# Fused dilated sliding-window attention and GEGLU block: loads, output copies, masks and the first gate stage put in another order

## The chip, the core and the metric

The kernel runs on one core of a Trainium2 chip. The core has five engines with an instruction stream each: TensorE (PE in the profile, its weight loads PEld), VectorE (DVE), ScalarE (ACT), GpSimd (POOL) and SyncE (SP), which here only issues transfers. Each works through its stream in order and waits on semaphores for the others. The metric is the device time of one execution in microseconds (us).

## What is computed

For 8 batches and 8 heads of 576 positions with head size 64, a softmax attention is taken in which a query sees only a few keys: heads 0 to 3 ("plain") the last 32 positions, heads 4 to 7 ("dilated") every fourth of the last 128. The result, 4608 tokens by 512, goes through a gated feed-forward block.

```python
rel = pos[:, None] - pos[None, :]
mask_plain = (rel >= 0) & (rel < 32)
mask_dil = (rel >= 0) & (rel < 128) & (rel % 4 == 0)
scores = np.where(mask, q @ k.T / 8, -1e9)
attn = softmax(scores);  x = attn @ v            # x: 4608 x 512
out = (gelu(x @ w_gate) * (x @ w_val)) @ w_out   # 512 -> 1536 -> 512
```

## The kernel before, in words

The whole order is written by hand (`manual_schedule`): each engine runs its instructions in the order in which the code names them, and the frame only adds the semaphore waits.

**Attention units.** A unit `n` is a pair of heads of one batch, four units to a batch: `n // 4` is the batch, units 0 and 1 of a batch are plain, 2 and 3 dilated. A unit has three steps. `emit_s` computes the scores on PE into four PSUM banks starting at `b0`, then ACT takes the exponential into a tile `P` (L329 and L330 for a plain unit, L345 for a dilated one). The mask is applied in one of two ways: with `pe_mask=True`, PE first adds a bias of 0 or -60000 by four matmuls with the identity (L315, L335); otherwise `emit_s` hands back a function that multiplies `P` by a 0/1 mask on DVE (L353). `emit_pv` computes, on PE, the numerators and the denominators (L435; `den` and `num` do the two apart). `norm_r` (transpose L440, reciprocal L442, transpose L444) makes the reciprocals on DVE, and `norm_x` (L455 plain, L458 dilated) writes the unit's 128 rows of x, transposed, into `xT[n % 4]`.

**Feed-forward chunks.** The 4608 tokens are nine chunks of 512. Chunk `c` first runs twelve column blocks `nb` of `ffn1`: four matmuls for the gate, four for the value (L470), one for each of the four `xT` tiles; `geglu` then takes the gelu on ACT (L495) and the product on DVE (L496). The first two blocks of chunks 0 to 2 go through `ffn1_two`, which in the kernel before runs `xT[0..2]` for both blocks (gate and value) and then `xT[3]` for all four sums (L483). Then come four token blocks of `ffn2`, twelve matmuls each (L502), whose sums `store` copies to SBUF (`osb`, L513 on ACT) and sends out (L517 on SP). `osb` has four buffers. `hooks` put attention steps between the matmuls of an `ffn2`.

**PSUM.** Eight banks. `mm0` (0, later 4) is the first of the four banks of the feed-forward, `SB = 4 - mm0` the first of the four in which scores are made, `V = mm0 + 1` the first bank of a unit's numerators and denominators in chunks 0 to 2. All scores of a chunk use the same four banks, so a unit's scores wait until the exponential of the unit before them has read its own.

**Which unit where.** `in_a` gives the units whose `emit_pv` lies among the `ffn1` blocks of a chunk, `in_b` those whose scores lie from the last `ffn1` block on. The scores of batch 2 lie in chunk 1, those of batches 3 and 4 in chunks 1 and 2, and of batch `c + 2` at the end of chunk `c` from chunk 3 on. Units 20 and 24, the first of batches 5 and 6, thus open the `ffn2` part of chunks 3 and 4.

**Loads.** `load_batch` of a batch issues, on SP, 15 loads of q, k (L183) and v (L171), then seven DMA transposes ("the crossbar": L212, L213, L217) into `qTd` and `qTp`; and on POOL, loads of the dilated part (L196 to L206) and the casts to 16 bits (L188, L189, L175, L176) that the transposes wait for. SP works in order, so transposes that wait for a cast hold up all that stands behind them, outputs too. The tile `st`, and the 16-bit copies `qp`, `qd` and `rd`, have one buffer each. Batches 0 and 1 come another way: their q and k are transposed on PE (`t_plain` L258, `t_dil` L279 and L289) and copied out of PSUM (L243 ACT, L247 DVE).

Of the kernel before, what the change touches and what calls it, by code (L numbers as in the profile page):

```python
# [37 lines left out]
def kernel(  # L38
# [436 lines left out]
    def ffn1_two(c, pairs):  # L475

        tok = slice(c * CH, (c + 1) * CH)
        for kcs in (range(NKC - 1), (NKC - 1,)):
            for nb in range(2):
                ns = slice(nb * P, (nb + 1) * P)  # L480
                for gi, w in ((0, wg_t[0]), (1, wv_t[0])):
                    for kc in kcs:
                        nc.tensor.matmul(  # L483
                            ps[:, pairs[nb] + gi, :],
                            w[:, kc, ns],
                            xT[kc][:, tok],
                            start=(kc == 0),
                            stop=(kc == NKC - 1),
                        )
# [63 lines left out]
    for hp in range(2):  # L553
        t_plain(0, q6, hp, 2 * hp, ("act", "dve"))
    copy("pool", qd0[:, 0], r4(first_d[0]))
    copy("dve", qd0[:, 1], r4(first_d[1]))
    nc.vector.tensor_scalar(bias_d, mask_d, 1.0, 60000.0, ALU.subtract, ALU.mult)
# [15 lines left out]
    emit_s(0, 4, pe_mask=True)  # L573
    emit_s(1, 0, pe_mask=True)
    warm(2, 7)
    t_dil(0, 0, qd0, first_r, 4, 0, ("dve", "dve", "dve"))
    t_dil(0, 1, qd0, first_r, 4, 1, ("act", "dve", "dve"))
    den(0, 5)
    emit_s(2, 0, pe_mask=True)
    den(1, 5)  # L580
# [32 lines left out]
    in_a = {2: ((3, 12), (7, 13)), **{c: tuple(zip((1, 3, 5, 7), range(NHP * (c + 1), NHP * (c + 2)))) for c in range(3, B - 1)}}  # L613
    in_b = {1: range(8, 14), 2: range(14, 20), **{c: range(NHP * (c + 2), NHP * (c + 3)) for c in range(3, B - 2)}}
    for c in range(NCH):
        if c == 1:
            load_batch_rest(2, *half2)
        if c >= 2 and c + 2 < B:
            load_batch(c + 2)
        pv_at = dict(in_a.get(c, ()))  # L620
# [6 lines left out]
        for nb in range(NNB):  # L627
# [4 lines left out]
            elif nb > 1 or c > 2:  # L632
                ffn1(c, nb, pairs[(nb + (c < 2)) % 2])
# [7 lines left out]
            if c == 0 and nb in (6, 7):  # L641
                t_plain(1, q61, nb - 6, 4 + 2 * (nb - 6), ("act", "dve"))
            if c == 0 and nb == 8:
                rr = rd1.rearrange("p t h r d -> p t (h r d)")
                for hp in range(2):
                    t_dil(1, hp, qd1, (rr[:, 0], rr[:, 1]), 4, hp, ("dve", "dve", "dve"))
# [124 lines left out]
```

## Time and profile before

| | us |
|---|---|
| three runs, lowest / median / highest | 378.22 / 379.12 / 382.39 |
| the profiled execution, device time | 378.81 |
| its span, first to last instruction | 377.0 |
| PE busy in it | 350.3 |
| DVE / ACT / POOL busy | 196.4 / 148.5 / 68.1 |

In PE's timeline the chunks' first matmuls stand at 26.1 us (chunk 0), 75.7 (1), 116.9 (2), 158.8 (3), 197.9 (4) and 238.9 (5). A row of the timeline has the start, the duration, the engine, the line, the operation, what it writes and reads, how many were merged, and in brackets how long the engine stood idle just before and which instruction or transfer ended that. Since matmuls overlap, the step of a stream of them is read from their starts: eight of an `ffn1` block take 1.73 us, twelve of an `ffn2` block 2.59.

### The profile page before, as it was taken

How to read it: one execution, taken by the hardware profiler on the slowest of the kernel's cores; microseconds unless marked ns; L12 is line 12 of the kernel's file. 1: busy time of each engine (PE TensorE's matmuls, PEld its weight loads, DVE VectorE, ACT ScalarE, POOL GpSimd, SP SyncE). 2: the span in 40 equal slices, each digit the busy share in tenths (PEclk: the TensorE clock that was granted, in tenths of full speed). 3: DMA queues.
4: the chain of work that ended last, by engine and by line, in shares of the span. 5: the costliest groups of instructions: out<-in, count | busy, mean ns of one | idle time of the engine just before them, and what ended most of it. 6: DMA issues, size and time to landing. Idle time of an engine off the chain costs nothing.

```text
span 377.0 us, 6546 instructions
## 1 busy us (share of the span) xinstructions
PE 350.3 (93%) x2644; PEld 168.0 (45%) x2644; DVE 196.4 (52%) x293; ACT 148.5 (39%) x209; POOL 68.1 (18%) x94
## 2 busy tenths in 40 slices
PE   5969898999979999799799979999999999999995
PEld 2544444444434444354344434444444444444442
DVE  3593434644487665579427942497359704312420
ACT  2532356143636245622463244523653213313321
POOL 2380504520620520025000520040000000000000
PEclk9898999999999999999999998999999999999999
DMA  8999999969994991189618981488110020011002
GB/s 208 221 172 230 159 201 188 183 126 189 192 182 127 179 150 60 54 191 140 81 57 198 157 112 56 125 176 103 57 57 0 2 83 30 0 57 57 0 28 83
DMA packets 101565, 44.04 MB, mean 117 GB/s; under 512 B 76768, under 2 KB 96752, under 8 KB 101536
## 3 DMA queue, kind: packets, MB, share of 16 engines
q1 hardware_dynamic: 82224, 30.69, 37.9%
q0 software_dynamic: 17776, 11.25, 23.2%
q10 hardware_dynamic: 1536, 1.70, 2.0%
q8 instruction: 20, 0.33, 0.4%
q14 instruction: 9, 0.07, 0.1%
HBM read 38.05 MB, written 9.44 MB: 126 GB/s over the span
## 4 chain that ended last, share of the span: by engine, by line
PE 58%; DMA 17%; SPq 12%; DVE 4%; issue 3%; POOL 3%; ACT 2%; ACTq 0%; POOLq 0%; DVEq 0%
PE ps L470 27%; PE ps L502 23%; SPq L217 6%; DMA qTp<-qp 5%; SPq L183 4%; DMA st<-in_k_dram 4%; PE ps L435 4%; DMA xT<-in_k_dram 3%; DMA sv<-in_v_dram 3%; DMA wv<-in_moe_w_val_dram 2%; PE ps L343 1%; PE ps L326 1%; SPq L171 1%; POOL vp L175 1%; DVE xT L458 1%
## 5 line engine op out<-in xcount | busy, mean ns | idle before, releaser
L495 ACT ACTIVATE g<-ps 128x512 f16<-128x512 f32 x108 | 64.0, 597 | 141.3 <-PE ps L470 129.9
L496 DVE SCALAR_TENSOR_TENSOR u_all<-g,ps 128x512 f16<-128x512 f16 x108 | 73.9, 687 | 81.9 <-PE ps L470 69.2
L470 PE MATMUL ps<-xT,wg 128*128 128x512 f16 x408 | 104.9, 379 | 1.5 <-ACT osb L513 1.3
L502 PE MATMUL ps<-wo,u_all 128*128 128x512 f16 x432 | 101.4, 384 | 4.1 <-ACT osb L513 2.1
L470 PE MATMUL ps<-xT,wv 128*128 128x512 f16 x408 | 104.7, 379 | 0.1
L502 PEld LDWEIGHTS <-u_all 128*128 128x128 f16 x432 | 40.2, 99 | 52.5 <-issue 7.4
L470 PEld LDWEIGHTS <-wv 128*128 128x128 f16 x408 | 39.9, 98 | 48.5 <-issue 0.4
L470 PEld LDWEIGHTS <-wg 128*128 128x128 f16 x408 | 38.1, 98 | 46.9 <-issue 2.3
L188 POOL CAST qp<-st 128x2048 f16<-128x2048 f32 x6 | 11.3, 1890 | 122.3 <-DMA st<-in_k_dram 92.1
L513 ACT ACTIVATE osb<-ps 128x512 f32<-128x512 f32 x30 | 17.9, 597 | 36.0 <-PE ps L502 36.0
L440 DVE STREAM_TRANSPOSE dt<-ps 128x576 f32<-128x576 f32 x32 | 25.0, 780 | 10.1 <-PE ps L435 9.9
L345 ACT ACTIVATE P<-ps 128x1280 f16<-128x1280 f32 x16 | 19.8, 1236 | 17.1 <-PE ps L343 17.1
L444 DVE STREAM_TRANSPOSE rb<-rc 128x576 f32<-128x576 f32 x32 | 24.9, 778 | 1.1
L353 DVE TENSOR_TENSOR P<-P,mask_p 128x1440 f16<-128x1440 f16 x12 | 11.4, 956 | 22.4 <-ACT P L330 22.4
L515 DVE TENSOR_SCALAR osb<-ps 128x512 f32<-128x512 f32 x6 | 4.1, 691 | 30.6 <-PE ps L502 30.6
L329 ACT ACTIVATE P<-ps 128x800 f16<-128x800 f32 x16 | 13.4, 837 | 16.3 <-PE ps L326 16.2
L458 DVE TENSOR_TENSOR xT<-ps,rb 128x576 f16<-128x576 f32 x16 | 17.9, 1124 | 1.4 <-PE ps L435 1.1
L353 DVE TENSOR_TENSOR P<-P,mask_d 128x1280 f16<-128x1280 f16 x12 | 9.9, 823 | 15.6 <-ACT P L345 15.6
L435 PE MATMUL ps<-P,ones 128*64 128x64 f16 (+4 forms) x320 | 15.2, 224 | 0.6 <-DVE qTd L247 0.4
L326 PE MATMUL ps<-qTp 64*128 64x160 f16 (+1 forms) x160 | 9.0, 237 | 5.1 <-DMA qTp<-qp 5.1
L455 DVE TENSOR_TENSOR xT<-ps,rb 128x576 f16<-128x576 f32 x16 | 12.0, 751 | 2.7 <-PE ps L435 2.5
L175 POOL CAST vp<-sv 128x1024 f16<-128x1024 f32 x8 | 9.0, 1125 | 14.4 <-DMA sv<-in_v_dram 14.4
(71 smaller groups left out, 233.0 us busy)
## 6 DMA issues: line engine op xcount, KB each, us to landing
out_dram<-osb SPq DMA_DIRECT2D x36, 256.0 KB, 2.0
sv<-in_v_dram SPq DMA_DIRECT2D x32, 128.0 KB, 3.6
st<-in_q_dram SPq DMA_DIRECT2D x24, 128.0 KB, 3.1
st<-in_k_dram SPq DMA_DIRECT2D x24, 128.0 KB, 3.5
qd<-in_q_dram POOLq DMA_DIRECT2D x7, 256.0 KB, 5.1
qd<-in_k_dram POOLq DMA_DIRECT2D x7, 256.0 KB, 6.6
vd<-in_v_dram POOLq DMA_DIRECT2D x7, 256.0 KB, 6.3
wg<-in_moe_w_gate_dram POOLq DMA_DIRECT2D x3, 512.0 KB, 6.4
```

What stands on the lines that cost most here:

```text
L217: nc.sync.dma_start_transpose(out=dst[:, :, kb * P : kb * P + n], in_=qp[0:n, kb].rearrange("p t h d -> p (t h d)"))
L345: nc.scalar.activation(pt, ps[:, b0 : b0 + 4, 0:DW], AF.Exp, bias=0.0, scale=scale)
L353: nc.vector.tensor_tensor(pt, pt, mb, ALU.mult)
L435: nc.tensor.matmul(o, lhs, rhs, start=st, stop=True, skip_group_check=True)
L440: nc.vector.transpose(dt.rearrange("p b c -> p (b c)"), den)
L444: nc.vector.transpose(rb.rearrange("p (b c) -> p b c", c=32), bass.AP(tensor=rc.tensor, offset=rc.offset, ap=[rc.ap[0], [1, 18], [0, 32]]),)
L458: nc.vector.tensor_tensor(dst.rearrange("p (i m s) -> p i m s", m=2, s=2), num, rb.rearrange("p (s m i) -> p i m s", s=2, m=2), ALU.mult,)
L470: nc.tensor.matmul(ps[:, b0 + gi, :], w[:, kc, ns], xT[kc][:, tok], start=(kc == 0), stop=(kc == NKC - 1))
L495: nc.scalar.activation(g, ps[:, b0, :], AF.Gelu)
L496: nc.vector.scalar_tensor_tensor(u_all[:, nb, :], g, USCALE, ps[:, b0 + 1, :], ALU.mult, ALU.mult)
L502: nc.tensor.matmul(ps[:, bank, :], u_all[:, fc, tb * P : (tb + 1) * P], wo_t[fc // 4][:, fc % 4, :], start=(fc == 0), stop=(fc == NNB - 1),)
L513: nc.scalar.activation(osb, ps[:, bank, :], AF.Copy, bias=0.0, scale=1.0 / USCALE)
```

## The change

- The start. `bias_d` is computed on POOL instead of DVE, ahead of POOL's cast of `qd0`; in the built program a row named ISA stands directly ahead of it. The cast of the dilated k of batch 0 moves from DVE to ACT, between the exponentials of units 0 and 1, and four of the copies of `t_dil` go to ACT where three were on DVE. `den(0, 5)` moves ahead of the `t_dil` calls, `den(1, 5)` behind them and ahead of the scores of unit 2; two warming matmuls go.
- `ffn1_two` runs each `xT[kc]` for all four sums before the next `kc`.
- Chunk 0. The transposes of batch 1 move from blocks 6 to 8 to blocks 8 to 11. The scores of unit 4 move from block 10 to the middle of the first `ffn2`. Batch 1 is masked on DVE, without the bias matmuls.
- Loads. The second half of batch 2's load moves from the top of chunk 1 to before the first `ffn2` of chunk 0. Batch 3 is loaded at the top of chunk 1 instead of its block 4, batch 6 at block 5 of chunk 3 instead of the top of chunk 4, batch 7 at the top of chunk 4 instead of 5. Batches 4 and 5 stay at the top of chunks 2 and 3.
- Chunks 1 and 2. The scores of a unit come after the `store` of an `ffn2`, instead of in the middle of it, which puts the output copy ahead of the exponential on ACT; the mask of the next unit is queued on DVE between a unit's `emit_pv` and its `norm`. The scores of unit 13 move from chunk 1 to chunk 2, and the `emit_pv` of unit 13 from chunk 2's `ffn1` to its `ffn2`. Chunk 3 swaps the two pairs of banks of its blocks.

```diff
-        for kcs in (range(NKC - 1), (NKC - 1,)):
+        for kc in range(NKC):
             for nb in range(2):
                 for gi, w in ((0, wg_t[0]), (1, wv_t[0])):
-                    for kc in kcs:
-                        nc.tensor.matmul(
+                    nc.tensor.matmul(
...
+    nc.gpsimd.tensor_scalar(bias_d, mask_d, 1.0, 60000.0, ALU.subtract, ALU.mult)
     copy("pool", qd0[:, 0], r4(first_d[0]))
-    copy("dve", qd0[:, 1], r4(first_d[1]))
-    nc.vector.tensor_scalar(bias_d, mask_d, 1.0, 60000.0, ALU.subtract, ALU.mult)
...
     emit_s(0, 4, pe_mask=True)
+    copy("act", qd0[:, 1], r4(first_d[1]))
     emit_s(1, 0, pe_mask=True)
-    warm(2, 7)
-    t_dil(0, 0, qd0, first_r, 4, 0, ("dve", "dve", "dve"))
-    t_dil(0, 1, qd0, first_r, 4, 1, ("act", "dve", "dve"))
     den(0, 5)
+    for hp in range(2):
+        t_dil(0, hp, qd0, first_r, 4, hp, ("act", "act", "dve"))
+    den(1, 5)
     emit_s(2, 0, pe_mask=True)
-    den(1, 5)
...
-        if c == 1:
-            load_batch_rest(2, *half2)
-        if c >= 2 and c + 2 < B:
+        if c in (1, 2, 3):
             load_batch(c + 2)
+        if c == 4:
+            load_batch(7)
...
-                ffn1(c, nb, pairs[(nb + (c < 2)) % 2])
+                ffn1(c, nb, pairs[(nb + (c < 2 or c == 3)) % 2])
...
-            if c == 1 and nb == 4:
-                load_batch(3)
-            if c == 0 and nb == NNB - 2:
-                emit_s(NHP, SB, pe_mask=True)
+            if c == 3 and nb == 5:
+                load_batch(6)
...
+        def md(n, d):
+            mask_next()
+            den(n, d)
         if c == 0:
-            ffn2(c, 0, 0, {4: [lambda: s_den(5, 4)], 8: [lambda: s_den(6, 5)]})
+            load_batch_rest(2, *half2)
+            ffn2(c, 0, 0, {5: [s_next]})
             store(c, 0, 0, "act")
-            ffn2(c, 1, 1, {2: [lambda: s_den(7, 6)], 10: [lambda: s_den(None, 7)]})
+            ffn2(c, 1, 1, {4: [s_next, lambda: md(4, V)]})
             store(c, 1, 1, "act")
-            ffn2(c, 2, 0, {9: [lambda: num(4, 4)]})
+            s_next()
+            md(5, V)
+            ffn2(c, 2, 0, {7: [s_next, lambda: md(6, V)]})
             store(c, 2, 0, "act")
-            ffn2(c, 3, 1, {3: [lambda: num(5, 6)], 9: [lambda: num(6, 2)]})
+            ffn2(c, 3, 1, {4: [lambda: num(4, 4)], 9: [lambda: md(7, V), lambda: num(5, 6)]})
+            store(c, 3, 1, "act")
+            num(6, 2)
             num(7, 4)
-            store(c, 3, 1, "act")
...
-        elif c == 2:
-            ffn2(c, 3, mm0, {2: [s_next], 10: [s_next]})
+            ffn2(c, 3, mm0, {2: [lambda: pv(v0 + 2)], **({8: [s_next]} if c == 2 else {})})
             store(c, 3, mm0, "act")
+            s_next()
+            if c == 1:
+                pv(v0 + 3)
+            else:
+                s_next()
```

How three engines' instructions stand. In the rows, `st` and `sv` are the 32-bit loads, `qTd` and `qTp` the transposed tiles, `osb` the outputs, and a number behind a name tells buffers apart.

SP at the border of chunks 3 and 4, before: the last transposes of batch 5, the outputs of chunk 3, then the loads of batch 6.

```order
L217 DMA_TRANSPOSE qTp_1921<-qp_1918 128x4x128 x4
L217 DMA_TRANSPOSE qTp_1921<-qp_1918 128x4x64
L517 DMA out_dram<-osb 128x512 x4
L183 DMA st_2316<-in_q_dram 128x4x64 x4
L183 DMA st_2316<-in_q_dram 64x4x64
L183 DMA st_2316<-in_k_dram 128x4x64 x4
L183 DMA st_2316<-in_k_dram 64x4x64
```

The same place now:

```order
L217 DMA_TRANSPOSE qTp_1907<-qp_1904 128x4x64
L183 DMA st_2078<-in_q_dram 128x4x64 x4
L183 DMA st_2078<-in_q_dram 64x4x64
L183 DMA st_2078<-in_k_dram 128x4x64 x4
L183 DMA st_2078<-in_k_dram 64x4x64
L171 DMA sv_2091<-in_v_dram 128x4x64 x4
L171 DMA sv_2091<-in_v_dram 64x4x64
L212 DMA_TRANSPOSE qTd_2107<-qd_2097 128x16x128
L213 DMA_TRANSPOSE qTd_2107<-rd_2098 128x16x16
L217 DMA_TRANSPOSE qTp_2106<-qp_2103 128x4x128 x4
L217 DMA_TRANSPOSE qTp_2106<-qp_2103 128x4x64
L516 DMA out_dram<-osb 128x512 x4
```

All of batch 6 has moved ahead of the four outputs of chunk 3. The transposes of batch 2 and the outputs of chunk 0 have changed places in the same way.

ACT at the end of chunk 2, before: the exponentials of units 16 to 19 among the output copies (`osb`), up to the gelu of chunk 3.

```order
L329 ACTIVATE P_1759<-ps 128x2x400
L330 ACTIVATE P_1759<-ps 128x2x320
L513 ACTIVATE osb<-ps 128x512
L329 ACTIVATE P_1819<-ps 128x2x400
L330 ACTIVATE P_1819<-ps 128x2x320
L513 ACTIVATE osb<-ps 128x512
L345 ACTIVATE P_1858<-ps 128x1280
L345 ACTIVATE P_1884<-ps 128x1280
L513 ACTIVATE osb<-ps 128x512
L495 ACT_TABLE_LOAD
```

The same place now:

```order
L512 ACTIVATE osb<-ps 128x512
L329 ACTIVATE P_1777<-ps 128x2x400
L330 ACTIVATE P_1777<-ps 128x2x320
L329 ACTIVATE P_1830<-ps 128x2x400
L330 ACTIVATE P_1830<-ps 128x2x320
L512 ACTIVATE osb<-ps 128x512
L345 ACTIVATE P_1856<-ps 128x1280
L345 ACTIVATE P_1874<-ps 128x1280
L494 ACT_TABLE_LOAD
```

The copy of each output stands ahead of the exponential that was ahead of it, and the exponentials of units 18 and 19 now follow the last output copy of the chunk.

DVE in the `ffn2` part of chunk 0, before: the reciprocals of unit 7, then the rows of x of units 4 and 5.

```order
L444 STREAM_TRANSPOSE rb<-rc 128x576
L440 STREAM_TRANSPOSE dt<-ps 128x576
L442 RECIPROCAL rc<-dt 128x18
L444 STREAM_TRANSPOSE rb<-rc 128x576
L455 TENSOR_TENSOR xT_99<-ps,rb 128x576
L455 TENSOR_TENSOR xT_100<-ps,rb 128x576
```

The same place now:

```order
L353 TENSOR_TENSOR P_808<-P_808,mask_d 128x1280
L440 STREAM_TRANSPOSE dt<-ps 128x576
L442 RECIPROCAL rc<-dt 128x18
L444 STREAM_TRANSPOSE rb<-rc 128x576
L455 TENSOR_TENSOR xT_99<-ps,rb 128x576
L353 TENSOR_TENSOR P_852<-P_852,mask_d 128x1280
L440 STREAM_TRANSPOSE dt<-ps 128x576
L442 RECIPROCAL rc<-dt 128x18
L444 STREAM_TRANSPOSE rb<-rc 128x576
L455 TENSOR_TENSOR xT_100<-ps,rb 128x576
```

Each unit's mask now stands between the reciprocals of the unit before it and its own denominators, which PE can only compute once the mask is done.

71 lines of the change are left out of this document (24 added, 47 removed).

## The prediction

> **What bounds the kernel now.** I read the page first, then PE's waits, then PE's timeline at each wait, then what the releaser was doing.
>
> ```profile
> span 377.0 us, 6546 instructions
> PE 350.3 (93%) x2644; PEld 168.0 (45%) x2644; DVE 196.4 (52%) x293; ACT 148.5 (39%) x209; POOL 68.1 (18%) x94
> ...
> PE ps L326 <- DMA qTp<-qp: 5.1, 3, 2.2
> PE ps L502 <- ACT osb L513: 2.1, 3, 0.7
> PE ps L483 <- DVE xT L458: 2.0, 2, 1.5
> PE ps L470 <- ACT osb L513: 1.3, 1, 1.3
> PE ps L435 <- DVE xT L455: 0.9, 1, 0.9
> ```
>
> PE is busy for 93% of the span, and no other engine passes 52%: PE's order is the critical path, and time can only come from its 26.7 us of waits, from work it need not do, and from its clock. The waits are short and scattered. The clock shows in the busy time by stretches (columns: stretch, its length, busy time of PE, PEld, DVE, ACT, POOL with counts, granted clock, DMA share, GB/s):
>
> ```profile
> 24.80:28.20 3.40, 0.91 (x18) 0.51 (x13) 3.33 (x6) 0.00 (x0) 2.87 (x6) 1.00 1.22 197
> 28.20:31.60 3.40, 3.38 (x9) 1.15 (x9) 1.00 (x1) 0.00 (x0) 0.44 (x1) 0.50 1.24 207
> 181.80:185.20 3.40, 1.82 (x12) 0.60 (x9) 1.33 (x2) 1.88 (x2) 0.00 (x0) 1.00 0.92 106
> 222.80:226.20 3.40, 1.23 (x11) 0.63 (x12) 0.53 (x1) 1.66 (x3) 0.00 (x0) 1.00 0.37 32
> 226.20:229.60 3.40, 3.40 (x10) 1.23 (x9) 0.91 (x1) 0.58 (x1) 0.00 (x0) 0.50 0.00 0
> ```
>
> Stretches in which PE worked only 0.91 and 1.23 us are each followed by 3.4 us at half clock, one with 1.82 us is not. Each half-clock stretch costs 1.7 us. So a wait can cost more than itself, if it falls badly.
>
> ```profile
> 26.10 0.59 PE L483 MATMUL ps<-xT,wg 128*128 128x512 f16 x2 [0.98 <-DVE dt L440]
> 28.22 0.58 PE L483 MATMUL ps<-xT,wg 128*128 128x512 f16 x1 [1.53 <-DVE xT L458]
> 43.20 0.43 PE L258 MATMUL ps<-ident,qp 96*128 96x96 f16 x6 [1.24 <-POOL qp L245]
> 48.78 0.71 PE L279 MATMUL ps<-ident,qd 128*128 128x128 f16 x8 [0.45 <-DVE qTd L247]
> 57.82 1.02 PE L502 MATMUL ps<-wo,u_all 128*128 128x512 f16 x4 [1.61 <-ACT g L495]
> 158.76 1.02 PE L470 MATMUL ps<-xT,wg 128*128 128x512 f16 x4 [1.29 <-ACT osb L513]
> 185.64 0.35 PE L326 MATMUL ps<-qTp 64*128 64x80 f16 x6 [2.02 <-DMA qTp<-qp]
> 185.92 3.84 PE L502 MATMUL ps<-wo,u_all 128*128 128x512 f16 x17
> 224.97 0.35 PE L326 MATMUL ps<-qTp 64*128 64x80 f16 x6 [2.18 <-DMA qTp<-qp]
> 225.25 5.53 PE L502 MATMUL ps<-wo,u_all 128*128 128x512 f16 x17
> ```
>
> Those are the places. Seventeen matmuls take 3.84 us, so about 0.2155 each, 0.86 for four; behind the 2.18 us wait the same seventeen take 5.53.
>
> **The change, part by part.** I follow PE from mark to mark.
>
> *Start, to block 2 of chunk 0: -1.3.*
>
> ```profile
> 13.96 0.98 DVE L247 CAST qd<-xT 128x1024 f16<-128x1024 f32 x1 [2.10 <-DMA xT<-in_k_dram]
> 16.35 0.58 ACT L243 COPY qTd<-ps 128x512 f16<-128x512 f16 x1 [0.74 <-PE ps L279]
> 18.60 0.51 PE L343 MATMUL ps<-qTd 64*128 64x144 f16 x16
> 27.08 2.12 DVE L458 TENSOR_TENSOR xT<-ps,rb 128x576 f16<-128x576 f32 x2
> ```
>
> The cast on ACT is not in the trace; at DVE's price (bounds 0.6 from ACT's 512-wide copy, 1.2 from twice that; 1.0 is nearest) it runs from 13.96 and pushes unit 1's exponentials from 14.2 to 15.0, done by 16.4. The first two of four ACT copies end at 17.6; only then may the second `t_dil` write, its last copy is off DVE by 19.0, then come `den(1)` (0.45) and the bias (0.65): unit 2's scores start at 20.15, not 18.60, 1.5 late. Everything behind, up to the two L458 that end at 28.15 and 29.2, slips by 1.5: PE's first gate matmul from 26.10 to 27.6, x[2] and x[3] to 29.65 and 30.75. Against that, by parts of x eight matmuls run before x[2] is needed (27.6 + 1.7 = 29.3), four follow it, and four follow x[3]: 31.6 at full clock, since PE now works some 2 us in the stretch to 28.2. Before it was 32.9 at half clock.
>
> *To the first `ffn2` of chunk 0: -4.7.* The transposes now come two blocks (3.45 us) later, at 43.7, past the cast that released 43.20: 1.24 gone. The two `t_dil` have a block between them: 0.45 gone. The exponential of unit 4 no longer puts a table load ahead of the last gelu: 1.61 and the issue of 0.1 around it gone. Unit 4's scores and bias (1.1) move into the next stage. `ffn2` starts at 51.8 instead of 57.8.
>
> *`ffn2` of chunk 0: +1.8.*
>
> ```profile
> 60.34 0.78 DVE L440 STREAM_TRANSPOSE dt<-ps 128x576 f32<-128x576 f32 x1 [1.86 <-PE ps L435]
> 61.11 0.85 PE L335 MATMUL ps<-bias_d,ident 128*128 128x320 f16 x4
> 61.46 0.78 DVE L444 STREAM_TRANSPOSE rb<-rc 128x576 f32<-128x576 f32 x1
> 70.89 0.76 DVE L455 TENSOR_TENSOR xT<-ps,rb 128x576 f16<-128x576 f32 x1 [1.10 <-PE ps L435]
> ...
> L353 DVE TENSOR_TENSOR P<-P,mask_p x12: 899/908/1507, 99.4 to 269.7; 128x1440 f16<-128x1440 f16 x12
> L353 DVE TENSOR_TENSOR P<-P,mask_d x12: 815/825/826, 105.9 to 274.7; 128x1280 f16<-128x1280 f16 x12
> ```
>
> Three bias groups at 0.7 go (-2.1), unit 4's scores come (+0.45). But each mask stands on DVE behind the reciprocals of the unit before: 1.9 us (60.34 to 62.24) plus 0.82 to 0.91, while PE has only eight to twelve matmuls and one set of scores (2.1 to 2.6 us less the 0.45 of `den`) to fill it. Worked along both queues, `den(5)`, `den(6)` and `den(7)` wait 0.75, 0.9 and 0.6, and chunk 1 waits 0.7 for unit 5's x, which now stands behind unit 7's reciprocals, to free bank 6. That is 2.95, with 0.5 for a mask that falls beside a POOL cast (the 1507 of the row above, once in twelve).
>
> *Chunk 1: -0.6.* Gone are, by the rows of PE's waits, one of the three on an output copy (0.7), the one on L455 (0.9), the third on `qTp` (5.1 less the 2.02 and 2.18 quoted: 0.9; the loads of batch 3 now start as soon as batch 2's transposes and four stores are issued, some 7 us earlier) and the second on L458 (0.5), 3.0 in all, and the scores of unit 13 (0.45); new are 0.35 twice for output copies, 0.4 for unit 8's x, 1.3 before unit 11 and 1.2 for its x behind a mask (3.6, less 0.8 that gaps of 0.1 around small groups, no longer on the path there, give back).
>
> *Chunk 2: +0.6.*
>
> ```profile
> 156.98 1.24 ACT L345 ACTIVATE P<-ps 128x1280 f16<-128x1280 f32 x1 [1.04 <-PE ps L343]
> 158.12 0.59 ACT L513 ACTIVATE osb<-ps 128x512 f32<-128x512 f32 x1
> ```
>
> Gone: the other two waits of 0.7 on output copies, and 1.29 at 158.76. New: 0.4 twice at output copies, 0.5 for unit 14's x, and at the end units 18 and 19 in one set of banks with only scores between: 18 waits 0.7 for exponential 17, 19 waits 1.24 plus 0.15 for exponential 18. That is 3.3 against 2.7. Chunk 3 starts 4.2 ahead, at 154.6.
>
> *Chunk 3: -1.8.*
>
> ```profile
> 159.12 2.81 SPq L183 DMA_DIRECT2D st<-in_q_dram  x5
> 172.29 8.18 SPq L217 DMA_TRANSPOSE qTp<-qp  x5
> ```
>
> Batch 5's loads stay behind chunk 2's last store. They began 2.1 after that chunk's last matmul (157.0) and 26.5 before unit 20 was released; now the copy waits for exponential 17 alone (0.65 past the last matmul), takes 0.6, and the loads begin 0.4 later, 1.65 after. The release is thus at 151.55 + 28.1 = 179.65 against 185.64: 6.0 ahead, 0.5 of the wait left.
>
> *Chunk 4: -3.9.* Batch 6 is now asked for straight behind batch 5's transposes, some 18 us earlier: 2.18 goes, and with it the 1.7 of half clock. From there nothing differs.
>
> Sum: -1.3 - 4.7 + 1.8 - 0.6 + 0.6 - 1.8 - 3.9 = -9.9, from the profiled 378.8: **369.0 us** (0.3 below the median of 379.12).
>
> **A rule against the trace.** The stretches of 0.91 and 1.23 us show half clock after a partly idle stretch. The Trainium skill, "TensorE: Matmul & The Clock Gate" (Part 1, "What's actually happening"), has the clock halved after a whole idle window of about 3.4 us; by that rule no wait here would halve it and neither 1.7 could be gained, 372.4 in all. The trace decides: a busy window halved it.
>
> **The rivals.**
> - *Half clock elsewhere.* The new 0.7 and 1.39 at the end of chunk 2 leave about 1.3 us of work in 3.4, near the 1.23; the start may stay at half clock too. For: those two rows. Against: the 1.82, and that the stretches must fall in step with the wait. One: 370.7; both: 372.4.
> - *POOL is late at the start.*
>
> ```profile
> mask_d<-mask_dil POOLq DMA_DIRECT2D x1, 80.0 KB, 7.9
> ...
> 13.36 1.03 POOL L245 CAST qd<-xT 128x1024 f16<-128x1024 f32 x1 [9.84 <-DMA xT<-in_q_dram]
> ```
>
> POOL stands idle for 9.84 us ahead of that cast, and the mask has landed by 10.9 (issued at 2.96). If the ISA row takes as long as that transfer (7.9) it is over at 11.5 from its place, and hidden; if it starts only with the mask's arrival, POOL's cast comes at 19.4, 6 late, of which 1.7 is covered, since ACT's copies cannot start before 16.4: 4.3, 373.3. The Trainium skill, "GPSIMD Engine Reference" (2.1, Instruction dispatch), gives the first call of a freshly loaded routine about 6 us, unseen in a profile; by that figure behind the mask's arrival the loss would be 2.3 and the time 371.3. No run here shows it yet.
> - *The masks cost PE nothing*, if the order on DVE leaves more room than I reckon: -3.1, 365.9. For: DVE's 52%. Against: its order.
> - *Batch 5's transposes land later*, because batch 6's loads now follow them at once on the same queue, where SP was idle from 180.5 (172.29 + 8.18): for, the transfers share their engines; against, the loads are behind them. Bounded by nothing and the old wait of 2.0 once more: 371.0.
> - *The waits on the transposes stay*, with the half clock: 369.0 + 2.2 + 1.7, and the start's 1.7: 374.6 to 376.3; within 1%.
> - *Slower: outputs run out of buffers.* Chunk 0's outputs now stand behind seven transposes on SP.
>
> ```profile
> 78.58 1.66 SPq L213 DMA_TRANSPOSE qTd<-rd  x1
> 100.48 0.60 ACT L513 ACTIVATE osb<-ps 128x512 f32<-128x512 f32 x1 [1.12 <-PE ps L502]
> ```
>
> Chunk 1's first output copy (100.5 before, some 4 earlier now) needs the first store to have landed. The transposes should be issued by 78; the time passes 378.8 only if they end 28 us later. Nothing points to it.
>
> **How the numbers follow.** Forecast 0.36, half clock 0.22, POOL late 0.12, masks free 0.10, batch 5 late 0.07, waits stay 0.09, outputs 0.04. The first five lie between 365.5 and 373.5, my range, 0.87 of the chance. About 1% (3.8 us) is what a measurement here can tell from no change: faster by more than that 0.87, within 0.09, slower 0.04.
>
> **What would show it.** Right: PE without a wait at L326 in chunk 4, full clock there, chunk 3 starting near 154.6, first `ffn2` near 51.8, `den` waits of 0.6 to 0.9 on the masks in chunk 0, about 1.4 before unit 19. Wrong: POOL's first cast well after 13.4, half clock at 28 or 152, or a wait for `qTp` of over 1 us.

## The result, and the profile after

| | before | after |
|---|---|---|
| runs, lowest / median / highest (us) | 378.22 / 379.68 / 382.39 | 369.02 / 369.78 / 369.96 |
| the profiled execution | 378.81 | 369.64 |
| its span | 377.0 | 367.8 |

The ratio of the times is 0.973 (95% interval 0.967 to 0.979); here and below ratios are taken over each kernel's fast runs, those within 1.5% of its fastest. The forecast was 369.0 in a range of 365.5 to 373.5.

The page of the profile after has in its first two lines the span and the engines' busy time:

```profile
span 367.8 us, 6517 instructions
PE 347.3 (94%) x2626; PEld 167.7 (46%) x2626; DVE 197.5 (54%) x292; ACT 147.9 (40%) x211; POOL 70.1 (19%) x95
```

PE's waits after (what waited, what released it: us in all, times, longest):

```profile
PE ps L435 <- DVE P L353: 1.9, 4, 0.6
PE ps L435 <- DVE xT L458: 1.6, 5, 0.9
...
PE ps L343 <- ACT P L345: 1.3, 1, 1.3
PE ps L482 <- DVE xT L458: 1.3, 2, 1.1
PE ps L482 <- DVE dt L440: 1.2, 1, 1.2
PE ps L501 <- ACT osb L512: 1.0, 4, 0.3
```

PE's busy time fell by 3.0 us, the span by 9.2. No wait on `qTp` is left, and the longest is now on exponentials, masks and x. The places in PE's timeline after that the prediction spoke of:

```profile
19.65 1.25 PE L335 MATMUL ps<-bias_d,ident 128*128 128x320 f16 x4
20.83 0.76 PE L343 MATMUL ps<-qTd 64*128 64x144 f16 x16
29.08 0.38 PE L482 MATMUL ps<-xT,wg 128*128 128x512 f16 x1 [1.24 <-DVE dt L440]
33.09 1.03 PE L470 MATMUL ps<-xT,wg 128*128 128x512 f16 x4
53.05 1.25 PE L501 MATMUL ps<-wo,u_all 128*128 128x512 f16 x5
61.06 0.50 PE L435 MATMUL ps<-P,ones 128*64 128x64 f16 x12 [0.50 <-DVE P L353]
64.25 0.47 PE L435 MATMUL ps<-P,ones 128*64 128x64 f16 x8 [0.63 <-DVE P L353]
69.00 0.47 PE L435 MATMUL ps<-P,ones 128*64 128x64 f16 x8 [0.60 <-DVE P L353]
72.11 0.38 PE L482 MATMUL ps<-xT,wg 128*128 128x512 f16 x1 [0.70 <-DVE xT L455]
75.56 1.03 PE L470 MATMUL ps<-xT,wg 128*128 128x512 f16 x4
115.71 0.38 PE L482 MATMUL ps<-xT,wg 128*128 128x512 f16 x1 [1.06 <-DVE xT L458]
153.83 0.76 PE L343 MATMUL ps<-qTd 64*128 64x144 f16 x16 [1.33 <-ACT P L345]
154.52 1.89 PE L470 MATMUL ps<-xT,wg 128*128 128x512 f16 x4
156.20 1.48 PE L470 MATMUL ps<-xT,wv 128*128 128x512 f16 x4
157.52 1.03 PE L470 MATMUL ps<-xT,wg 128*128 128x512 f16 x4
180.34 0.49 PE L326 MATMUL ps<-qTp 64*128 64x160 f16 x10
217.30 0.49 PE L326 MATMUL ps<-qTp 64*128 64x160 f16 x10
229.72 1.03 PE L470 MATMUL ps<-xT,wg 128*128 128x512 f16 x4
```

At 180.34 and 217.30 the scores of units 20 and 24 begin without a wait. At 154.52 eight matmuls take 3.0 us (157.52 less 154.52), where 1.73 is usual: half clock. The busy time by stretches shows it there and at the start (columns as in the prediction: length, PE, PEld, DVE, ACT, POOL, granted clock, DMA):

```profile
14.00:17.40 3.40, 2.11 (x24) 1.63 (x24) 2.02 (x4) 3.40 (x6) 1.72 (x3) 0.97 1.28 255
17.40:20.80 3.40, 3.02 (x26) 2.06 (x24) 1.30 (x3) 0.76 (x2) 2.18 (x3) 0.50 1.25 203
20.80:24.20 3.40, 3.04 (x29) 1.41 (x30) 0.82 (x2) 1.24 (x1) 3.40 (x6) 0.53 0.97 132
150.50:153.90 3.40, 1.69 (x22) 0.79 (x24) 2.74 (x4) 3.16 (x4) 0.00 (x0) 0.97 0.18 60
153.90:157.30 3.40, 3.40 (x23) 1.52 (x23) 1.56 (x2) 2.06 (x2) 0.00 (x0) 0.53 0.86 201
```

POOL's first two computations, on which one rival rested:

```profile
11.03 1.29 POOL L554 TENSOR_SCALAR bias_d<-mask_d 128x320 f16<-128x320 f16 x1 [7.50 <-DMA mask_d<-mask_dil]
13.12 1.04 POOL L245 CAST qd<-xT 128x1024 f16<-128x1024 f32 x1 [0.80 <-DMA xT<-in_q_dram]
```

With the same marks of before, each step of the prediction against what it measured (the change of the time from one mark to the next, worked out from the two timelines, of one execution each):

| up to | before | after | step | predicted |
|---|---|---|---|---|
| block 2 of chunk 0 | 32.91 | 33.09 | +0.2 | -1.3 |
| first `ffn2` of chunk 0 | 57.82 | 53.05 | -4.9 | -4.7 |
| block 2 of chunk 1 | 79.12 | 75.56 | +1.2 | +1.8 |
| block 2 of chunk 2 | 121.15 | 116.77 | -0.8 | -0.6 |
| chunk 3 | 158.76 | 154.52 | +0.1 | +0.6 |
| chunk 4 | 197.92 | 192.75 | -0.9 | -1.8 |
| chunk 5 | 238.93 | 229.72 | -4.0 | -3.9 |
| sum | | | -9.2 | -9.9 |

### The profile page after: what moved, and what is told of

Its sections match the earlier page's. It is cut to its first block, busy times and chain, and to the rows that moved or that the text cites. A ratio compares the mean times of both kernels' runs of the same rounds, so it can differ in the third digit from the quotient of the medians.

```text
span 367.8 us, 6517 instructions
## 1 busy us (share of the span) xinstructions
PE 347.3 (94%) x2626; PEld 167.7 (46%) x2626; DVE 197.5 (54%) x292; ACT 147.9 (40%) x211; POOL 70.1 (19%) x95
## 4 chain that ended last, share of the span: by engine, by line
PE 79%; DVE 11%; ACT 4%; DMA 3%; issue 1%; POOL 0%; SPq 0%; DVEq 0%; ACTq 0%
PE ps L470 45%; PE ps L501 23%; PE ps L435 5%; DMA xT<-in_q_dram 3%; DVE dt L440 2%; DVE xT L458 2%; DVE rb L444 2%; PE ps L482 2%; PE ps L343 2%; DVE u_all L495 1%; DVE P L353 1%; PE ps L326 1%; ACT P L345 1%; DVE rc L442 1%; DVE xT L455 1%
## 5 line engine op out<-in xcount | busy, mean ns | idle before, releaser
L470 PE MATMUL ps<-xT,wg 128*128 128x512 f16 x408 | 105.8, 382 | 0.5 <-ACT g L494 0.4
L501 PE MATMUL ps<-wo,u_all 128*128 128x512 f16 x432 | 99.6, 380 | 1.4 <-ACT osb L512 1.0
L353 DVE TENSOR_TENSOR P<-P,mask_p 128x1440 f16<-128x1440 f16 x14 | 13.1, 937 | 22.8 <-ACT P L330 22.8
L353 DVE TENSOR_TENSOR P<-P,mask_d 128x1280 f16<-128x1280 f16 x14 | 12.5, 890 | 13.5 <-ACT P L345 13.5
L435 PEld LDWEIGHTS <-ones 128*64 128x64 f16 x320 | 11.3, 113 | 3.6 <-issue 3.1
L482 PE MATMUL ps<-xT,wg 128*128 128x512 f16 x24 | 9.1, 379 | 3.2 <-DVE xT L458 1.3
```

The source lines that it names most:

```text
L353: nc.vector.tensor_tensor(pt, pt, mb, ALU.mult)
L435: nc.tensor.matmul(o, lhs, rhs, start=st, stop=True, skip_group_check=True)
L470: nc.tensor.matmul(ps[:, b0 + gi, :], w[:, kc, ns], xT[kc][:, tok], start=(kc == 0), stop=(kc == NKC - 1))
L482: nc.tensor.matmul(ps[:, pairs[nb] + gi, :], w[:, kc, ns], xT[kc][:, tok], start=(kc == 0), stop=(kc == NKC - 1),)
L501: nc.tensor.matmul(ps[:, bank, :], u_all[:, fc, tb * P : (tb + 1) * P], wo_t[fc // 4][:, fc % 4, :], start=(fc == 0), stop=(fc == NNB - 1),)
```

## The experiments

The kernel before was run beside each group of these. Its median was 378.47 beside the first four, 377.63 beside the next four and 377.68 beside the two after those, single runs 373.3 to 382.9. The kernels made from the changed one lie closer together, so their medians are set against its 369.8. The second four ran on another chip than the groups before and behind them, and no time of the changed kernel on that chip is on record, so a difference of 1 us or so in that group can be the chip's.

**The loads alone.** The kernel before with the four moved loads, nothing else:

```diff
-        if c == 1:
-            load_batch_rest(2, *half2)
-        if c >= 2 and c + 2 < B:
+        if c in (1, 2, 3):
             load_batch(c + 2)
+        if c == 4:
+            load_batch(7)
...
-            if c == 1 and nb == 4:
-                load_batch(3)
+            if c == 3 and nb == 5:
+                load_batch(6)
...
         if c == 0:
+            load_batch_rest(2, *half2)
```

> The kernel before with the loads alone moved as in the change (second half of batch 2 and batch 3 earlier, batch 6 inside chunk 3, batch 7 in chunk 4), nothing else. My step: in chunk 4 the 2.18 us wait for qTp goes and with it the 1.7 us of half clock behind it, in chunk 1 a wait of 0.9 us on qTp goes; unit 20 in chunk 3 still waits about 2.0 us. Together -4.8: about 374.0 to 374.9, ratio 0.987. Rival 1: the half clock is not the wait's doing (a busy window does not halve the clock); then -3.1 and half clock still near 226. Rival 2: the earlier loads of batch 6 hold up the transposes of batch 5; then unit 20 waits longer than 2.0 and the gain is under 3.

Measured: 371.54 (371.13 to 373.85), ratio 0.987 (0.980 to 0.994), which is the gain of some 5 us that was expected. Between the two profiled executions it is more, since the last PE instruction is 7.4 earlier: 1.1 in chunk 1, 2.1 at unit 20, and 4.1 between unit 24 and chunk 5. Chunk 4 did as I said: no wait, and full clock in 222 to 226 and after it. So rival 1 falls, since the half clock went with the wait. So does rival 2, by PE's timeline of this run:

```profile
182.08 0.55 PE L326 MATMUL ps<-qTp 64*128 64x160 f16 x10
```

In this row of PE's timeline unit 20, too, waits for nothing, which I had not expected. Batch 5's transposes had landed at 182.1, 24.2 us after its first load was issued (157.90); in the profile before it took 26.4, in that after 26.8. The time that a batch takes from load to landing thus differs by over 2 us between executions, and why is open; it is also why this profile gained more than expected.

**The start as before, the gate stage by parts of x.**

```diff
-    nc.gpsimd.tensor_scalar(bias_d, mask_d, 1.0, 60000.0, ALU.subtract, ALU.mult)
     copy("pool", qd0[:, 0], r4(first_d[0]))
+    copy("dve", qd0[:, 1], r4(first_d[1]))
+    nc.vector.tensor_scalar(bias_d, mask_d, 1.0, 60000.0, ALU.subtract, ALU.mult)
...
-    copy("act", qd0[:, 1], r4(first_d[1]))
     emit_s(1, 0, pe_mask=True)
-    den(0, 5)
-    for hp in range(2):
-        t_dil(0, hp, qd0, first_r, 4, hp, ("act", "act", "dve"))
-    den(1, 5)
+    warm(2, 7)
+    t_dil(0, 0, qd0, first_r, 4, 0, ("dve", "dve", "dve"))
+    t_dil(0, 1, qd0, first_r, 4, 1, ("act", "dve", "dve"))
+    den(0, 5)
     emit_s(2, 0, pe_mask=True)
+    den(1, 5)
```

> The changed kernel with the start as before (k cast and bias_d on DVE, t_dil ahead of den(0), copies mostly on DVE, two warming matmuls), but the first gate stage by parts of x. Theory: the re-ordered start is a loss in itself (first gate matmul 26.1 before, 29.1 in the changed kernel, half clock from 17.4 to 24.2), and the order by parts of x alone takes away the half clock at 28.2: block 2 of chunk 0 then starts at about 30.3 instead of 33.1, and the time is about 2.8 less than the changed kernel's: 366.8. Rival: the half clock at 28.2 stays, whichever order the gate stage has; then block 2 starts at 32 to 33 and the time is 368.5 to 369.6. Rival: the new start is what the later steps need (DVE free earlier); then slower than 369.6.

Measured: 368.90 (368.52 to 369.27), 0.9 less than the changed kernel; block 2 of chunk 0 at 31.43 instead of 33.09, and no half clock at 28. So the new start is a loss of 1.7 by itself, and the order by parts of x does what was said of it. But of the 1.7 only 0.3 is left at the end of this execution. Most was given back at the end of chunk 1, as PE's timeline of this run shows:

```profile
109.45 0.35 PE L326 MATMUL ps<-qTp 64*128 64x80 f16 x6 [0.73 <-DMA qTp<-qp]
115.22 0.38 PE L482 MATMUL ps<-xT,wg 128*128 128x512 f16 x1 [1.38 <-DVE xT L458]
```

Unit 12's scores now came ahead of batch 3's transposes, which landed at 109.3 in this execution and at 107.3 in that of the changed kernel, so the later landing took the gain as much as the earlier scores did. Unit 12's exponential and its mask then came later, and unit 11's x, which stands behind that mask on DVE, too (1.38 instead of 1.06). Another 0.4 went in chunk 3, where the stretch at half clock (here 154.0 to 157.4) is still there.

**The gate stage in the old order.** `ffn1_two` as in the kernel before, the rest as changed.

> The changed kernel with the first gate stages in the old order (parts 0 to 2 of x for both blocks, then part 3). Theory: only two matmuls can run ahead of part 2 of x, so PE works under 1 us in the stretch to 31.0 and half clock follows: block 2 of chunk 0 starts at about 35.5 instead of 33.1, and the time is 2 to 3 more: about 372. In chunk 2 nothing is late before part 3, so nothing changes there. Rival: the order of these sixteen matmuls only moves a wait; then 0.3 to 1.0 more: 370.2.

Measured: 371.88 (371.49 to 374.05), 2.1 more than the changed kernel. The profiled execution has block 2 of chunk 0 at 36.12; the busy time by stretches ahead of it:

```profile
28.44:31.85 3.41, 1.02 (x5) 0.38 (x4) 3.34 (x6) 0.00 (x0) 1.12 (x2) 1.00 1.24 208
31.85:35.26 3.41, 3.41 (x10) 1.21 (x9) 0.55 (x1) 0.00 (x0) 0.00 (x0) 0.50 1.23 208
```

The wait for part 2 of x leaves 1.02 us of work in a stretch, and half clock follows. The order of sixteen matmuls is worth 3 us there.

**The end of chunk 2 spread.**

```diff
-            ffn2(c, 2, mm0, {4: [lambda: pv(v0 + 1)]})
+            ffn2(c, 2, mm0, {4: [lambda: pv(v0 + 1)], **({6: [s_next]} if c == 2 else {})})
...
-            ffn2(c, 3, mm0, {2: [lambda: pv(v0 + 2)], **({8: [s_next]} if c == 2 else {})})
+            ffn2(c, 3, mm0, {2: [lambda: pv(v0 + 2)], **({6: [s_next]} if c == 2 else {})})
             store(c, 3, mm0, "act")
             s_next()
             if c == 1:
                 pv(v0 + 3)
                 mm0 = 4 - mm0
-            else:
-                s_next()
```

> The changed kernel with the scores of units 16 to 19 each one place earlier at the end of chunk 2, so that units 18 and 19 no longer stand next to each other. Theory: the waits of 0.38 and 1.33 us ahead of units 18 and 19 shrink to some 0.5 in all, PE works over 2.3 us in the stretch before 153.7, the half clock from 153.9 to 157.3 goes (1.5), and chunk 3's second block starts about 2.8 earlier: 366.9. Rival 1: the half clock falls elsewhere or stays, because it is not the wait that causes it: about 368.4. Rival 2: exponentials queued ahead of output copies give the waits back on osb: 369 to 370.

Measured: 369.50 (366.97 to 372.22). Where it was made it did as I said: chunk 3 started at 152.09 instead of 154.52, and without half clock. Then, in PE's timeline of this run:

```profile
179.64 0.35 PE L326 MATMUL ps<-qTp 64*128 64x80 f16 x6 [2.68 <-DMA qTp<-qp]
```

and in its busy time by stretches:

```profile
176.78:180.19 3.41, 0.73 (x12) 0.33 (x9) 0.69 (x1) 1.19 (x2) 0.00 (x0) 1.00 1.42 172
180.19:183.60 3.41, 3.41 (x10) 1.17 (x9) 0.91 (x1) 1.25 (x2) 0.00 (x0) 0.50 1.36 212
```

Batch 5's transposes landed at 179.5, as in the changed kernel (179.6), since its loads stand behind chunk 2's last output in both. There unit 20 came 0.7 after them; here it came 3 us before, and its wait brought the half clock along. Neither rival had this floor: the landing is a floor for all that is gained ahead of it. The four runs spread over 5 us and only this one was profiled; the lowest, 366.97, is the time expected without such a wait.

**The floor moved: the spread, and batch 5 loaded in chunk 2.** The next run takes the spread and this edit, the one after it this edit alone:

```diff
-        if c in (1, 2, 3):
+        if c in (1, 2):
             load_batch(c + 2)
...
-            if c == 3 and nb == 5:
-                load_batch(6)
+            if c in (2, 3) and nb == 5:
+                load_batch(c + 3)
```

> The scores at the end of chunk 2 spread as in the run of that name, and batch 5 loaded at block 5 of chunk 2 instead of the top of chunk 3. Theory: what gave the gain back there was the landing of batch 5's transposes at 179.5, tied to chunk 2's last output; loaded earlier they are there by 165, unit 20 waits for nothing, the half clock at 180.2 is gone, and the last PE instruction stands at about 360.1 instead of 363.8: 366.0 us. Rival: batch 5's transposes now stand ahead of chunk 2's outputs on SP and wait for unit 15's scores; if the four output buffers run out, PE waits at chunk 3's output copies and the time is 369 or more.

Measured: 366.97 (365.35 to 367.96), 2.8 less than the changed kernel. Unit 20 waits for nothing and there is no half clock at 154 or 180. The output buffers did not run out. Its last PE instruction is 1.7 earlier, not 3.7, because in this execution unit 12 met batch 3's landing, at 111.4 instead of 107.3, though no load ahead of it was moved (PE's timeline):

```profile
111.50 0.35 PE L326 MATMUL ps<-qTp 64*128 64x80 f16 x6 [1.25 <-DMA qTp<-qp]
117.26 0.38 PE L482 MATMUL ps<-xT,wg 128*128 128x512 f16 x1 [1.38 <-DVE xT L458]
```

> The changed kernel with only batch 5 loaded at block 5 of chunk 2. Theory: unit 20 stood at 180.34 and its transposes landed at 179.62, so nothing was waiting for them: no change, 369.0 to 370.0, the same marks up to chunk 3. Rival: the casts of batch 5 on GpSimd now fall among the masks of chunk 2 on VectorE and slow one or two of them by 0.6 each: 370.3 to 371.

Measured: 368.40 (367.86 to 372.39), 1.4 less than the changed kernel, somewhat below what no change would give. In the profiled execution the marks agree with those of the changed kernel to 0.4 up to chunk 3. Unit 19 then waits the same 1.33, but a stretch of the clock begins at 152.8, as that wait begins, and holds 2.08 us of PE work; no half clock follows. The busy time of that stretch:

```profile
152.80:156.21 3.41, 2.08 (x30) 1.10 (x24) 1.61 (x3) 2.69 (x4) 0.00 (x0) 1.00 1.41 206
```

The early load itself cost and gained nothing that shows.

**The blocks of chunk 0 as before.**

```diff
-            if c == 0 and nb in (8, 9):
-                t_plain(1, q61, nb - 8, 4 + 2 * (nb - 8), ("act", "dve"))
-            if c == 0 and nb in (10, 11):
+            if c == 0 and nb in (6, 7):
+                t_plain(1, q61, nb - 6, 4 + 2 * (nb - 6), ("act", "dve"))
+            if c == 0 and nb == 8:
                 rr = rd1.rearrange("p t h r d -> p t (h r d)")
-                t_dil(1, nb - 10, qd1, (rr[:, 0], rr[:, 1]), 4, nb - 10, ("dve", "dve", "dve"))
+                for hp in range(2):
+                    t_dil(1, hp, qd1, (rr[:, 0], rr[:, 1]), 4, hp, ("dve", "dve", "dve"))
+            if c == 0 and nb == NNB - 2:
+                masks.append(emit_s(s_list.pop(0), SB))
...
-            ffn2(c, 0, 0, {5: [s_next]})
+            ffn2(c, 0, 0)
```

> The changed kernel with batch 1's transposes back behind blocks 6 to 8 of chunk 0 and unit 4's scores back behind block 10 (masked on VectorE). My step: the cast wait (1.24), the copy wait (0.45), the table load ahead of the last gelu (1.6) come back, and unit 4's scores move (0.45): first ffn2 of chunk 0 at 56.9 instead of 53.05, chunk 1 3.4 later, about 373.0. Rival: the cast is there earlier now, so only the table load counts: first ffn2 at 55.2, 371.3.

Measured: 374.80 (372.67 to 378.42), 5.0 more than the changed kernel. The waits came back, and larger, in PE's timeline of the profiled execution:

```profile
44.66 0.43 PE L258 MATMUL ps<-ident,qp 96*128 96x96 f16 x6 [3.19 <-POOL qp L245]
60.93 3.61 PE L501 MATMUL ps<-wo,u_all 128*128 128x512 f16 x16 [2.22 <-ACT g L494]
```

The busy time by stretches around the first of them:

```profile
42.45:45.86 3.41, 1.21 (x11) 0.73 (x12) 0.74 (x1) 0.00 (x0) 2.09 (x3) 1.00 1.06 156
45.86:49.27 3.41, 3.41 (x20) 1.78 (x19) 1.36 (x3) 1.24 (x2) 2.98 (x5) 0.50 0.49 57
```

The profiled execution is the longest of the four (378.42). In it the cast wait is 3.19, and half clock follows it. The first `ffn2` comes at 60.93, against 56.9 expected. Behind a wait of 1.79 for a mask, at 69.46, a second stretch runs at half clock, which I had not foreseen. The waits are those that were named. Their price is shown by this one execution alone: batch 1's k was there for the casts at 43.8, against 42.3 in the profile before and 41.9 in that after, and what the other three runs paid for each wait is not known.

**The masks of chunk 0 on TensorE again.** In the hooks of chunk 0, `emit_s` with `pe_mask=True`, and `mask_next` has nothing to do.

> The changed kernel with batch 1 masked by the bias matmuls on TensorE again (four groups at 0.7 us, 2.8 more work), the masks on VectorE gone. Theory: the waits of den on the masks (1.9 in all) and most of the 0.7 before chunk 1 go, so chunk 0's ffn2 part is 0.2 to 0.9 longer: 369.8 to 370.5. Rival: by the prediction's own step (3.45 of waits against the bias) it would be 0.65 shorter: 369.0.

Measured: 368.69 (367.96 to 372.91). From the first `ffn2` to chunk 1 it takes 19.2 us against 19.1: the bias matmuls (about 2.8) and the waits for masks cost the same here. All it gains comes 80 us later, in a place that the edit does not touch (PE's timeline):

```profile
154.57 0.51 PE L343 MATMUL ps<-qTd 64*128 64x144 f16 x16 [1.33 <-ACT P L345]
155.02 1.04 PE L470 MATMUL ps<-xT,wg 128*128 128x512 f16 x4
```

Unit 19 waits the same 1.33, but no half clock follows: the clock's stretch ended at 154.3 here, and held 1.99 us of PE work where that of the changed kernel held 1.7:

```profile
150.88:154.29 3.41, 1.99 (x30) 0.95 (x27) 2.98 (x4) 2.92 (x4) 0.00 (x0) 1.00 0.07 25
```

**All of it together.** The start as before, the spread, batch 5 in chunk 2, and two more edits:

```diff
     def load_batch(b):
-        load_batch_rest(b, *load_batch_plain(b))
+        st = load_qk_plain(b)
+        sv = new_v(b)
+        qd, rd = load_qk_dil(b)
+        qp = cast_qk_plain(b, st)
+        crossbar(b, qp, qd, rd)
+        v_plain(b, sv, nc.sync)
+        load_v_dil(b)
+        v_cast(b, sv)
...
-                pv(v0 + 3)
+                emit_pv(v0 + 3, V)
+                norm(v0 + 3, V)
```

> All that the runs so far point to, in one kernel made from the changed one: the start as before with the gate stage by parts of x, the scores at the end of chunk 2 spread, batch 5 loaded in chunk 2, a batch's v loaded behind its transposes (so that batch 3's transposes, which held unit 12 up by 0.5 to 1.3 us in the last runs, land some 2 us earlier), and unit 11's reciprocals ahead of unit 12's mask on VectorE. Theory: block 2 of chunk 0 at about 31.4 (1.7 less; 1.2 of it kept past chunk 1), chunk 2 started 0.7 less late for unit 11's x, end of chunk 2 2.4 shorter and no half clock behind it (1.3): 5.5 less than the changed kernel, 364.2. Rival: each gain meets the next landing (unit 12's or unit 20's transposes) and is given back: 366.5 to 367, as in the run with only the spread and batch 5.

Measured: 364.58 (363.28 to 366.01), ratio to before 0.968 (0.963 to 0.973). The changed kernel beside it:

> The changed kernel itself, timed beside the combined one on the same chip: 369.0 to 370.5. Where the half clock falls should differ between its executions, since stretches that come near the limit (the start, the end of chunk 2) fall differently on the clock's 3.41 us stretches each time.

Measured: 369.85 (369.04 to 370.53), ratio 0.981 (0.976 to 0.985). The combined kernel is 5.3 us faster than the changed one; what each of its edits gave was not measured apart. In its profiled execution, the fastest of the six, units 12, 20 and 24 wait for no transposes. With v behind the transposes, batch 3 took 22.1 us from its first load to the landing of its last transpose, against 25.2 to 28.4 in the eleven other profiles of the changed kernel or of kernels made from it. In its PE timeline (its lines from `load_batch` on are numbered 7 higher) stand what is left of the wait for unit 11's x, and chunk 3 without half clock:

```profile
112.35 0.38 PE L489 MATMUL ps<-xT,wg 128*128 128x512 f16 x1 [0.46 <-DVE xT L465]
148.48 0.51 PE L350 MATMUL ps<-qTd 64*128 64x144 f16 x16
149.48 1.02 PE L477 MATMUL ps<-xT,wg 128*128 128x512 f16 x4 [0.49 <-DVE xT L465]
```

The second execution of the changed kernel had its half clock at 154.3 instead of 153.7, and at the start a further one from 11.0 to 14.4, as expected of a clock whose stretches do not begin with the program.

**What the clock is granted by.** Two kernels with idle work added to the last chunks; nothing reads it.

```diff
+            if (c, nb) in ((5, 10), (6, 10), (7, 4), (7, 10), (8, 4)):
+                r, m = {(5, 10): (64, 128), (6, 10): (128, 64), (7, 4): (64, 64), (7, 10): (128, 32), (8, 4): (128, 128)}[c, nb]
+                for _ in range(48):
+                    nc.tensor.matmul(ps[0:m, 0, :], ones[0:r, 0:m], ones[0:r], start=True, stop=True)
```

> The changed kernel with 48 extra matmuls of 512 columns at each of five places in chunks 5 to 8, back to back, into a bank that nothing reads: 64 rows by 128 columns of the array, 128 by 64, 64 by 64, 128 by 32, and 128 by 128. PE is busy without a break in all five. Theory, from the traces so far: a stretch of 3.41 us is followed by half clock when the work in it, with each matmul counted by the share of the array that it uses, is under about 1.25 us; then the two halves (1.71 per stretch) and the full array stay at full clock, about 10.4 us each, and the two quarters (0.85) fall to half clock after their first stretch, about 17 us each: some 65 us more in all. Rival 1: busy time alone counts; then all five stay at full clock, 10.4 each, 52 more in all. Rival 2: only the rows in use count, or only the columns; then one of the halves and one of the quarters differ from their partners.

Measured: 423.38, 53.5 more than the changed kernel; all five at full clock, 10.5 each. My theory as it stood is wrong: a quarter of the array counts like the whole. The two quarters in PE's timeline:

```profile
332.46 10.54 PE L638 MATMUL ps<-ones 64*64 64x512 f16 x48
353.40 10.53 PE L638 MATMUL ps<-ones 128*32 128x512 f16 x48
```

```diff
+            if (c, nb) in ((7, 4), (7, 10), (8, 4)):
+                w = {(7, 4): 16, (7, 10): 64, (8, 4): 32}[c, nb]
+                for _ in range(240):
+                    nc.tensor.matmul(ps[:, 0, 0:w], ones[:, 0:P], ones[:, 0:w], start=True, stop=True)
```

> The changed kernel with 240 extra matmuls of the whole array, back to back, at each of three places in chunks 7 and 8: with 16, 64 and 32 columns each, into a bank that nothing reads. The narrow stretches have shown that the share of the array does not count. What is left of my theory: the clock is granted by the time in which columns stream (512 columns in 0.2155 us, so 0.0067 us for 16, 0.027 for 64), and half clock follows a stretch of 3.41 us with under about 1.25 us of it, however busy PE looks. If a short matmul takes about 0.06 us, as in the first transposes, 16 columns stream for 11% and 32 for 22% of the time and fall to half clock, while 64 stream for 45% and stay at full clock. Rival: busy time or the number of matmuls counts; then all three stay at full clock.

Measured (one execution, 391.70): the matmuls took 6.22, 7.16 and 6.16 us, so a short one takes 0.026 and not 0.06. The busy time by stretches has one filled by matmuls of 16 columns, the one behind it, and one filled by matmuls of 32:

```profile
313.57:316.98 3.41, 3.41 (x143) 3.41 (x140) 0.00 (x0) 0.00 (x0) 0.00 (x0) 1.00 0.02 5
316.98:320.39 3.41, 3.41 (x54) 1.98 (x51) 0.00 (x0) 0.39 (x1) 0.00 (x0) 0.50 0.00 0
357.95:361.36 3.41, 3.41 (x144) 3.41 (x140) 0.30 (x1) 0.00 (x0) 0.00 (x0) 1.00 0.02 5
```

In the first PE is busy without a break, yet half clock follows; in the third it is as busy, with as many matmuls, and it does not. So neither busy time nor the number decides, as far as one execution can show. By 0.2155 us for 512 columns, columns streamed in the first for 0.9 us and in the third for 1.8. That 32 columns would fall to half clock was wrong, since the short matmuls came faster than I had reckoned.

## Why the prediction came out as it did

The time and its sign were right. The mechanism was right in five of the seven steps; the first failed, and the sixth was mis-sized. The time is nearer than the steps: these two missed by 1.5 and 0.9, and the other five came out 1.6 better in sum, so part of the agreement is luck.

- *Start (-1.3, measured +0.2).* The failed step is the slip of 1.5 ahead of the first gate matmul: it was 3.0 (29.08 against 26.10). The order of the waits was nearly right: unit 2's bias began at 19.65, where 19.5 was reckoned. But from 17.2 to 24.0 PE ran at half clock: the bias matmuls took 1.25 instead of 0.72, and unit 2's scores came at 20.83, not 20.15. I had taken half clock from the old place at 28 and not looked for a new one where PE waits for ACT's cast and copies (14.0 to 17.4). The trace before held a warning that I did not read: PE ran at half clock from 11.2 to 14.6, behind a stretch in which it was busy for 2.11. Over all profiles, the four with the old start have at most one stretch of 3.41 us at half clock ahead of the first gate matmul, which stands at 25.5 to 27.4; nine of the ten with the new start have two to four, and it stands at 28.4 to 30.1. A step of the start that is taken from two executions is thus sure to no better than 1 to 2 us. The gate stage itself was right: 4.0 us from its first matmul to block 2, as predicted, at full clock. The run with the old order has it 2.8 longer, the run with the old start begins block 2 at 31.43.
- *To the first `ffn2` (-4.7, measured -4.9).* The cast wait, the copy wait and the table load went; undoing them cost 5.0 in the median. The terms given for this step add up to 4.5, not 4.7.
- *`ffn2` of chunk 0 (+1.8, measured +1.2).* The `den` waits came on the masks as said, 0.50, 0.63 and 0.60 instead of 0.75, 0.9 and 0.6, and the wait of 0.7 before chunk 1. Two of the masks did fall beside a POOL cast (those of units 4 and 7, at 56.82 and 68.00), but took 0.91 and 0.95 us, so the 0.5 set aside for that was not spent.
- *Chunks 1 and 2 (0.0, measured -0.7).* The wait ahead of unit 19 was 1.33 for 1.39. The waits for output copies were 0.24 to 0.27, not 0.35 to 0.4, that ahead of unit 11 was 0.91, not 1.3, and that for its x 1.06, not 1.2.
- *Chunk 3 (-1.8, measured -0.9).* Batch 5's transposes landed at 179.62; 179.65 was predicted. To agree so closely is luck, since from load to landing this batch took 24.0 to 27.5 us in the eleven profiles in which its loads open chunk 3. All of the old wait went, 2.0; by the prediction's own numbers (2.0 less 1.8) 0.2 of it would be left, not the 0.5 that it says. The mis-sized term is the half clock behind unit 19, which the prediction had only as a rival: 1.3 of it lies in chunk 3.
- *Chunk 4 (-3.9, measured -4.0).* Right, and the loads alone gave 4.1 there.

Of the rivals, half clock elsewhere came true at the end of chunk 2, one of the places that were to show the prediction wrong; at the start it came too, but from 17.2 to 24.0, while the rival had it stay at 28. Its own figure for both, 372.4, was 2.8 too high: each half clock cost about 1.5 instead of 1.7, and the other steps came out some 2.3 better in sum. POOL was not late: its first cast stood at 13.12, `bias_d` at 11.03. The waits on the transposes did not stay, and outputs did not run out of buffers. That batch 5's transposes would land later did not happen either. The masks are not free, but cost about as much as the bias matmuls.

The rule that I weighed, of the Trainium skill's "TensorE: Matmul & The Clock Gate" (Part 1, "What's actually happening"), has the clock halved after a whole idle window. If idle means without busy time, the traces disagree: here half clock followed windows in which PE was partly busy, and in the last run one of 3.41 us with 3.41 of busy time. The same section has the windows run freely, 3413 ns each, not beginning with the kernel. With that the traces agree: the half-clock stretches that the program's end does not cut off last 3.41, 6.83 or 10.24 us, whole numbers of such windows, and for the changed kernel one begins at 153.7 in one execution and 154.3 in the next.

What the change is worth in all is known less well than its forecast suggests: 9.9 us between the medians of the first result, 7.8 between those of the last group, where the kernel before ran ten times. By parts: the loads alone, in the kernel before, come within 1.7 us of the changed kernel (371.54 against 369.85, on the same chip). The order by parts of x is worth 2.1 and the blocks of chunk 0 5.0, each by what it costs to undo it; they are not additive, because a gain ahead of a landing is kept only as far as the landing lets it. The new start costs 1.7 in its place.

## What to carry to other kernels

Where one engine is the critical path, the times at which loads land are floors on it: a gain ahead of a floor is worth no more than the slack at it (0.7 us at unit 20 here), so find the next floor, and what holds its loads back, before shortening anything. A wait of some 1 us on TensorE can cost twice that by the clock, and whether it does depends on where it falls; spread short waits, and put matmuls whose operands are ready ahead of those that wait. Profile a kernel more than once before trusting a step of under 2 us.

## What the hardware showed unexpectedly

- A busy TensorE can lose its clock. Count the time in which columns stream (0.2155 us for 512), with the attention's matmuls on half of the array counted half, because they start in pairs: in the profile before, two of 160 columns start at 107.03 and the next two 0.07 later, which is the time of 160 columns once. In all fourteen profiles, after the first 33 us, the stretches of 3.41 us that were followed by half clock held 1.26 us or less, and those that were not held 1.28 and more. Where in its row a matmul's streaming is set moves the two figures, at most to 1.33 and 1.36, but they keep apart. The limit thus lies at an estimated 37 to 40% of the stretch. Busy time does not part them: a stretch with 1.84 of it was followed by half clock, one with 1.74 was not. In the first 33 us the count does not hold: half clock followed on some 1.5 us (1.0 of it transposes; the profile before, from 7.7) and did not on some 1.1 (the run with short matmuls, from 26.9). Why is open.
- The same wait (unit 19's 1.33) was followed by half clock in both profiled executions of the changed kernel, and by none in that with other masks and in that with batch 5 alone moved, by where the stretches began.
- From the first load of batch 5 to the landing of its last transpose 24.0 to 27.5 us went by in the eleven profiles in which these loads open chunk 3. In the two profiles of the changed kernel itself batch 3's transposes landed at 107.3 and 109.1, and in one with the same loads ahead of them at 111.4. A floor of this kind moves by 2 to 4 us by itself.
